# Decoding the weights in place, scaling the first output weights once, and pooling q and k of eight pairs on TensorE

## The chip, the core and the metric

The kernel runs on one core of a Trainium2 chip. The metric is the device time of one execution in microseconds (us), the median of the runs. Engines are named as the profile names them: PE is TensorE (PEld its weight loads), DVE VectorE, ACT ScalarE, POOL GpSimd, and SP the engine that issues the DMAs (SPq its queue). TensorE's clock has two levels, 1.2 and 2.4 GHz; the profile gives the granted clock as a share of the higher one.

## What is computed

Three steps follow one another: an attention over 4 batches of 8 heads, whose output becomes 2304 tokens of 512 numbers, and two MLPs (called moe) of 512 to 2048 to 512.

```python
def _attn_ref(q, k, v):                       # (4, 8, 576, 64)
    ...
    q_d = q.reshape(B, H, Sd, factor, D).mean(axis=3)      # factor 4, Sd 144
    k_d = k.reshape(B, H, Sd, factor, D).mean(axis=3)
    v_d = v.reshape(B, H, Sd, factor, D).mean(axis=3)
    out_d = sm_attn(q_d, k_d, v_d)            # softmax(q k^T / 8) v
    out_up = np.repeat(out_d, factor, axis=2)
    mask = np.abs(pos[:, None] - pos[None, :]) < factor
    scores = np.where(mask, scale * np.matmul(q, k.transpose(0, 1, 3, 2)), -1000000000.0)
    ...                                       # softmax over the masked scores
    return (out_up + np.matmul(attn, v)).astype(np.float32)

def _moe_ref(x, w_in, w_out):
    h = x @ w_in
    g = np.maximum(h, 0.0) + np.log1p(np.exp(-np.abs(h)))
    return (g @ w_out).astype(np.float32)

def _moe2_ref(x, w_in, w_out):
    h = x @ w_in
    g = h * np.cos(h)
    return (g @ w_out).astype(np.float32)
```

## The kernel before

**Attention.** The heads are taken two at a time: 16 pairs (b, c), b the batch and c a pair of heads. `pair` (L525) writes one pair as a chain of named operations. qk, vd and vw are its loads (L528, L531, L533). sum1 and sum2 pool q and k by fours on DVE, into `qt` and then `qd`; sum3 and sum4 pool v, in place in `vd` and then into `vs`. A are the masked local scores on PE, A2 to A6 their softmax on DVE and ACT (`nm`, `sm`, `rs`). B are the scores of the pooled heads (three fp32 matmuls, L630), B1 to B4 their softmax, with B1a a scaling of the maximum `nd`. C and D are transposes on PE into PSUM, copied to `aT` and `aTd`; E are the products with v; up and E1 add the two outputs into `xt`, the tokens of the next step.

**MLPs.** Every fp32 operand is split into a high and a low f16 half after a scaling by powers of two, and each product is three f16 matmuls (high by high, high by low, low by high). L1 is x by w_in of the first MLP (L897, weights `w1i`), L2 its g by w_out (L989, `w1o`), L3 and L4 the same of the second (L897 with `w2i`, L1031 with `w2o`). Tokens go in five tiles, four of 512 and one of 256, and each tile through 16 units f of 128 hidden channels; a unit is 12 L1 or L3 matmuls, a chain of activations on ACT and DVE (`ta`, `tb`, `td`, `g`), and 12 L2 or L4 matmuls that add into two PSUM banks. L2 and L4 of a unit follow `LAG` = 4 units later (8 for the last tile).

**Weights.** They come as float64 bit patterns, in eight blocks b of 1024 columns for each of the four matrices. `Weight.decode` takes a block: a load into one of two staging buffers `stg` (L440, 1 MB), rebase on ACT (L453), join1 and join2 on DVE (L339 and L461) into one of three buffers `x`, and bound on ACT (L467), which gives each row's maximum in `bd`. join2 is the last reader of `stg`, bound writes a throw-away copy into the place of the high halves. `Weight.scale` spreads `bd` over all partitions (a matmul with an identity on PE, L378, and a reduction on DVE, L385) and finds the power of two by a few small steps on DVE; `Weight.split` writes the high half (L354 on ACT or L356 on DVE) and the low half (L350 on DVE). W1I and both matrices of the second MLP are scaled block by block. W1O is scaled in four groups of two blocks; so the first tile of L2 is accumulated in four parts, which `y_out` adds up on DVE (L1011).

**Scale of a tile.** Before a tile enters L1 or L3, its largest value is spread in the same way (`tile_scale`, `am`), and the four pieces of `xt` are split (`split_x`). In the second MLP `y_in(t)` does this at the start of tile t, and before tile 4 `drain(0)` empties the list of waiting L4 units.

**Order.** A planner (`Plan.due`, `Plan.order`) gives every operation a due time, going back from the end along the dependencies, and then lists the operations of each engine by due time and modelled cost; each engine executes its list in that order. While PE is idle in the plan, `filler` (L1195) puts zero matmuls there. Buffers in rings are given out in that order too, so a load waits on SP until its buffer is free.

Of the kernel before, what the change touches and what calls it, by code (L numbers as in the profile page):

```python
# [44 lines left out]
NQK, NVD, NVW, NSM, NXB, NST, NGS = 3, 2, 3, 3, 3, 2, 8  # L45
# [10 lines left out]
W2STEP = 1  # L56
# [27 lines left out]
class Plan:  # L84
# [36 lines left out]
    def due(self):  # L121
        nxt = 0.0
        for op in reversed(self.ops):
            e, cost = min(op.cost.items(), key=lambda x: x[1])
            end = min([s.due - LAT[e] for s in op.succ], default=0.0)
            if "pe" in op.cost:
                end = min(end, nxt)
                nxt = end - cost
            op.due = end - cost
# [26 lines left out]
    def order(self):  # L156
# [12 lines left out]
        def cool(cost, weight):  # L169

            if now < 0.6 or now > WARM:
                return False
            a0 = now + cost - WIN
            busy[:] = [b for b in busy if b[1] > now - WIN]
            return cost * weight + sum(max(0.0, b - max(a, a0)) * w for a, b, w in busy) < THR
# [91 lines left out]

def dma(kb):
    return {"sp": kb / 353.0}


def build(tc, qk, vw, vd, mask, w1i, w1o, w2i, w2o, out):
# [3 lines left out]
    with ExitStack() as ctx:  # L276
# [12 lines left out]
        def carr(name, n=1):  # L289
            return const.tile([128, n], F32, name=name)  # L290
# [6 lines left out]
        vmx = const.tile([128, NC_], F32, name="vmx")  # L297
# [17 lines left out]
        XB, STG = ring(dp, "x", NXB, [128, 2, 512]), ring(dp, "stg", NST, [128, 2, 512], I64)  # L315
# [52 lines left out]
        def allmax(am, n, red, reads, writes, name):  # L368
# [20 lines left out]
            P.add(pe(0.3 * n), spread, reads, [h], [h], name + " spread")  # L389
# [24 lines left out]
        class Weight:  # L414
            def __init__(self, name, dram):
                self.name, self.dram = name, dram
                self.w = [None] * NF
                self.bd, self.s = carr(f"bd_{name}", NB), carr(f"s_{name}", NF)

            def place(self, pool_):  # L420
                self.t = pool_.tile([128, NF, 2, 512], F16, name=f"{self.name}_t")

            def hi(self, f, a, n):
                return self.t[:, f, 0, a : a + n]

            def lo(self, f, a, n):
                return self.t[:, f, 1, a : a + n]
# [7 lines left out]
            def decode(self, b, after=()):  # L435

                raw, x = STG_.new(), XB_.new()
# [9 lines left out]
                def rebase():  # L447
# [6 lines left out]
                        out=x.t, in_=half(F32, 1), func=AF.Prelu, scale=float(2.0**-112), alpha=-float(2.0**32)  # L454
                    )

                def join1():
                    ts(bits(x.t), bits(x.t), 3, ALU.logical_shift_left)

                def join2():  # L460
                    nc.vector.scalar_tensor_tensor(  # L461
                        out=bits(x.t), in0=half(I32, 0), scalar=29, in1=bits(x.t),
# [9 lines left out]
                P.add(act(1024), rebase, [raw], [x], [x], nm + " rebase")  # L472
# [3 lines left out]
                return x  # L476
# [15 lines left out]
            def split(self, b, x):  # L492
                w, s = lambda: self.t[:, 2 * b : 2 * b + 2], self.s[:, 2 * b : 2 * b + 1]
                k = ("s", self.name, b)
# [5 lines left out]
                P.add(  # L500
                    dve(1024, False, 1), lambda: less("dve", w()[:, :, 1, :], x.t, s, w()[:, :, 0, :]),
                    [x, k], self.keys(b), name=nm + " low",
# [5 lines left out]
        STG_, XB_ = STG, XB  # L508
# [752 lines left out]
```

## Time and profile before

| what | before |
|---|---|
| median of 3 runs | 947.76 us (947.12 to 948.87) |
| the profiled execution | 947.95 us, span 946.2 us |
| granted clock of PE, mean | 0.986 |
| busy PE, DVE, ACT | 899.2, 690.4, 470.0 us |
| first L2 matmul, first L3 matmul | 173.70, 541.99 us |
| zero matmuls | 205, 53.07 us |

The span is the time from the first to the last instruction of the profiled execution. In the tables of windows a row is one stretch of it, with the busy time of each engine and the number of its instructions in brackets. Timelines list instructions, or runs of equal ones, with their start and length; in square brackets stand the idle time of the engine ahead of them and what ended it. A name with an arrow reads output<-inputs. Matmuls of fp32 leave two records each.

### The profile page before, as it was taken

How to read it: one execution, taken by the hardware profiler on the slowest of the kernel's cores; microseconds unless marked ns; L12 is line 12 of the kernel's file. 1: busy time of each engine (PE TensorE's matmuls, PEld its weight loads, DVE VectorE, ACT ScalarE, POOL GpSimd, SP SyncE). 2: the span in 40 equal slices, each digit the busy share in tenths (PEclk: the TensorE clock that was granted, in tenths of full speed). 3: DMA queues.
4: the chain of work that ended last, by engine and by line, in shares of the span. 5: the costliest groups of instructions: out<-in, count | busy, mean ns of one | idle time of the engine just before them, and what ended most of it. 6: DMA issues, size and time to landing. Idle time of an engine off the chain costs nothing.

```text
span 946.2 us, 14558 instructions
## 1 busy us (share of the span) xinstructions
PE 899.2 (95%) x5809; PEld 469.7 (50%) x5809; DVE 690.4 (73%) x1474; ACT 470.0 (50%) x823; POOL 1.6 (0%) x11
## 2 busy tenths in 40 slices
PE   7899887799999999999999999999999999999797
PEld 4555443345555554444446864444444444444364
DVE  7999999976668776999964566567557656755465
ACT  3464696525445467879866632234224323422243
POOL 0000000000000000000000000000000000000000
PEclk9999998899999999999999999999999999999899
DMA  9557332400122003442200000010001000100100
GB/s 312 164 168 243 119 128 89 171 26 27 31 64 104 1 1 118 152 175 89 90 1 1 1 2 0 1 42 4 1 1 45 1 1 1 45 1 1 44 1 23
DMA packets 13363, 58.89 MB, mean 62 GB/s; under 512 B 1520, under 2 KB 1648, under 8 KB 9200
## 3 DMA queue, kind: packets, MB, share of 16 engines
q1 hardware_dynamic: 13296, 57.97, 17.7%
q8 instruction: 45, 0.74, 0.3%
q14 instruction: 22, 0.18, 0.1%
HBM read 53.25 MB, written 4.72 MB: 61 GB/s over the span
## 4 chain that ended last, share of the span: by engine, by line
PE 74%; DVE 16%; ACT 6%; DMA 2%; issue 1%; SPq 0%; ACTq 0%; DVEq 0%
PE h L897 34%; PE any L1031 19%; PE any L989 17%; DVE td L350 1%; DVE x L461 1%; PE any L724 1%; DVE sm L342 1%; DVE w1i_t L350 1%; DMA vd<-vd 1%; ACT ta L905 1%; DVE xt L350 1%; DMA qk<-qk 1%; DVE rs L602 1%; PE any L675 1%; DVE g L342 1%
## 5 line engine op out<-in xcount | busy, mean ns | idle before, releaser
L897 PE MATMUL h<-xt,w2i_t 128*128 128x512 f16 (+1 forms) x960 | 201.5, 362 | 9.5 <-DVE xt L866 5.3
L897 PE MATMUL h<-xt,w1i_t 128*128 128x512 f16 (+1 forms) x960 | 199.4, 360 | 9.3 <-DVE red L385 6.6
L1031 PE MATMUL any<-w2o_t,g 128*128 128x512 f16 x864 | 197.1, 379 | 0.3 <-DVE g L362 0.3
L989 PE MATMUL any<-g,w1o_t 128*128 128x512 f16 (+1 forms) x864 | 179.5, 357 | 2.3 <-ACT ed L646 1.4
L897 PEld LDWEIGHTS <-w2i_t 128*128 128x128 f16 x960 | 95.3, 99 | 105.7 <-issue 11.5
L897 PEld LDWEIGHTS <-w1i_t 128*128 128x128 f16 x960 | 93.8, 98 | 102.6 <-issue 14.2
L989 PEld LDWEIGHTS <-w1o_t 128*128 128x128 f16 x960 | 93.7, 98 | 89.1 <-issue 4.8
L930 ACT ACTIVATE ta<-h,quarter,i 128x512 f32<-128x512 f32 (+1 forms) x80 | 58.8, 735 | 155.2 <-PE h L897 155.2
L1031 PEld LDWEIGHTS <-g 128*128 128x128 f16 x864 | 84.5, 98 | 100.6 <-DVE g L362 0.8
L342 DVE TENSOR_TENSOR g<-td,g 128x512 f16<-128x512 f32 (+1 forms) x152 | 96.3, 634 | 8.0 <-ACT g L360 1.3
L905 ACT ACTIVATE ta<-h,i 128x512 f32<-128x512 f32 (+1 forms) x80 | 51.4, 642 | 80.7 <-PE h L897 67.4
L935 DVE TENSOR_SCALAR tb<-ta 128x512 f32<-128x512 f32 (+1 forms) x80 | 32.0, 400 | 77.6 <-ACT ta L930 77.1
L945 DVE SCALAR_TENSOR_TENSOR td<-h,r,tc 128x512 f32<-128x512 f32 (+1 forms) x80 | 55.8, 697 | 42.9 <-ACT tc L941 41.2
L941 ACT ACTIVATE tc<-ta 128x512 f32<-128x512 f32 (+1 forms) x80 | 46.9, 586 | 74.5 <-DVE ta L342 74.5
L350 DVE SCALAR_TENSOR_TENSOR td<-ta,sg,tb 128x512 f32<-128x512 f32 (+1 forms) x64 | 43.7, 682 | 48.4 <-ACT ta L917 48.0
L917 ACT ACTIVATE ta<-ta,one 128x512 f32<-128x512 f32 (+1 forms) x80 | 54.2, 680 | 2.0
L362 DVE CAST g<-td 128x512 f16<-128x512 f32 (+1 forms) x124 | 49.4, 398 | 8.0 <-PE any L989 0.8
L342 DVE TENSOR_TENSOR ta<-ta,tb 128x512 f32<-128x512 f32 (+1 forms) x80 | 51.0, 638 | 2.4
L909 ACT ACTIVATE tb<-h,r 128x512 f32<-128x512 f32 (+1 forms) x80 | 51.1, 639 | 0.0
L913 ACT ACTIVATE ta<-ta 128x512 f32<-128x512 f32 (+1 forms) x80 | 46.9, 588 | 0.0
L453 ACT ACTIVATE x<-stg 128x1024 f32<-128x1024 f32 x32 | 36.8, 1149 | 14.1 <-DVE w2i_t L350 3.8
L1195 PE MATMUL h<-zero 128*128 128x512 f16 x133 | 34.4, 393 | 5.3 <-POOL zero L1186 2.4
(147 smaller groups left out, 848.8 us busy)
## 6 DMA issues: line engine op xcount, KB each, us to landing
qk<-qk SPq DMA_DIRECT2D x16, 589.0 KB, 6.6
stg<-w1i SPq DMA_DIRECT2D x8, 1024.0 KB, 7.0
stg<-w1o SPq DMA_DIRECT2D x8, 1024.0 KB, 6.4
stg<-w2i SPq DMA_DIRECT2D x8, 1024.0 KB, 4.8
stg<-w2o SPq DMA_DIRECT2D x8, 1024.0 KB, 4.8
vw<-vw SPq DMA_DIRECT2D x16, 320.0 KB, 4.3
vd<-vd SPq DMA_DIRECT2D x16, 288.0 KB
out<-osb SPq DMA_DIRECT2D x18, 256.0 KB, 2.1
```

Source lines behind the costliest of these rows:

```text
L342: eng[e].tensor_tensor(out=out, in0=in0, in1=in1, op=op)
L350: nc.vector.scalar_tensor_tensor(out=out, in0=raw, scalar=s, in1=other, op0=ALU.mult, op1=op)
L362: nc.vector.tensor_copy(out, in_)
L897: nc.tensor.matmul(h.t[:, 0:n], l, r, start=(i == 0), stop=(i == 11))
L905: act(n, 1, True), lambda: nc.scalar.activation(out=a(), in_=h.t[:, 0:n], func=AF.Abs, scale=col(o.i1, f)),
L909: act(n, 1, True), lambda: nc.scalar.activation(out=b(), in_=h.t[:, 0:n], func=AF.Relu, scale=col(o.r1, f)),
L913: act(n), lambda: nc.scalar.activation(out=a(), in_=a(), func=AF.Exp, scale=-1.0),
L917: act(n, 1), lambda: nc.scalar.activation(out=a(), in_=a(), func=AF.Ln, bias=one),
L930: act(n, 2, True), lambda: nc.scalar.activation(out=a(), in_=h.t[:, 0:n], func=AF.Identity, scale=col(o.i2, f), bias=quarter), [h, *sc], [ ...
L945: dve(n, False, 1), lambda: nc.vector.scalar_tensor_tensor(out=td.t[:, 0:n], in0=h.t[:, 0:n], scalar=col(o.r1, f), in1=r(), op0=ALU.mult, ...
L989: nc.tensor.matmul(a.t[:, i, 0:n], l, r, start=(first and j == 0), stop=(last and j == 2))
L1031: nc.tensor.matmul(a.t[:, i], l, r, start=(f == 0 and j == 0), stop=(f == NF - 1 and j == 2))
```

## The change

Weights are decoded in place. The f32 values of block b lie over the place of the low halves of block b and of the high halves of block b+1, in a tile that is one unit longer; the ring `x` is gone. bound's throw-away copy goes into the staging buffer, which is so given back after bound. The high of block b waits for the low of block b-1. W1I is scaled in two groups of four blocks. All eight blocks of W1O are decoded first and scaled once (`first_scale`), and the first tile of L2 is accumulated in one go. The second MLP's matrices are scaled in groups of two.

For batches 0 and 1 (eight pairs) q and k are pooled by PE: `sums`, eight fp32 matmuls with the identity for each pair, accumulated in PSUM, and `place`, three copies on ACT, the last with B1a's scale. The other pairs' B1a goes to ACT. Copies of the pairs of batches 0 and 1, the highs of W1I and W1O and of some x go to ACT always. The operands of the spreads become bf16.

In the second MLP the scale of tile t+1 is asked for at unit 8 of tile t, and before tile 4 four units stay in the list. The planner's due times take each engine's capacity into account, its costs are changed, and the zero matmuls come out as 82 instead of 205.

```diff
-W2STEP = 1
+W2STEP = 2
+W2G = 2
+QKP, VP = (0, 1), ()
+YIN = 8
+DR4 = 4
+A_W, A_C, A_X, A_G = True, True, True, False
+OUT0 = 10
+IN0 = ((0, 4), (4, 4))
...
-        ident_s = const.tile([128, 128], F32, name="ident_s")
+        ident_s = const.tile([128, 128], BF16, name="ident_s")
...
-                self.t = pool_.tile([128, NF, 2, 512], F16, name=f"{self.name}_t")
+                self.t = pool_.tile([128, 1024 * (NF + 1)], F16, name=f"{self.name}_t")
...
+            def floats(self, b):
+                return self.t[:, 2048 * b + 1024 : 2048 * b + 3072].bitcast(F32).rearrange("p (m e) -> p m e", m=2)
...
-                raw, x = STG_.new(), XB_.new()
+                raw, x = STG_.new(), ("float", self.name, b)
...
                 def bound():
-                    nc.scalar.activation(
-                        out=self.t[:, 2 * b : 2 * b + 2, 0, :].bitcast(BF16), in_=x.t, func=AF.Abs,
-                        accum_out=self.bd[:, b : b + 1],
-                    )
+                    out = raw.t.rearrange("p m e -> p (m e)")[:, 0:256].bitcast(BF16)
+                    with nc.allow_low_precision(reason="a bound, for the choice of a scale"):
+                        nc.scalar.activation(
+                            out=out.rearrange("p (m e) -> p m e", m=2), in_=self.floats(b), func=AF.Abs,
+                            accum_out=self.bd[:, b : b + 1],
+                        )
...
-                P.add(act(1024, 1), bound, [x], [("bd", self.name, b), *self.keys(b)], name=nm + " bound")
+                P.add(act(1024, 1), bound, [x], [("bd", self.name, b), raw], name=nm + " bound")
...
+                over = [("float", self.name, b - 1)] if b else []
                 P.add(
-                    {**act(1024, 1), **dve(1024, True, 1)}, lambda e: scaled(e, w()[:, :, 0, :], x.t, s),
-                    [x, k], self.keys(b), name=nm + " high",
+                    either(act(1024, 1), dve(1024, True, 1), self.first and A_W), lambda e: scaled(e, self.his(b), self.floats(b), s),
+                    [x, k], self.keys(b) + over, name=nm + " high",
                 )
...
+                def sums():
+                    x = tk.t[:, :, 3 : 3 + S].rearrange("p a (i r) -> p a i r", r=4)
+                    for a in range(2):
+                        for r in range(4):
+                            nc.tensor.matmul(
+                                hst()[:, SD * a : SD * a + SD], ident, x[:, a, :, r], start=(r == 0), stop=(r == 3)
+                            )
+
+                def place():
+                    for j in range(2):
+                        h = slice(64 * j, 64 * j + 64)
+                        copy("act", qd.t[h, SD * j : SD * j + SD], hst()[h, 0:SD])
+                    nc.scalar.activation(
+                        out=qd.t[:, 2 * SD : 3 * SD], in_=hst()[:, SD : 2 * SD], func=AF.Copy, scale=float(2.0**-7)
+                    )
...
-        def grp_out(g):
-            xs = [W1O.decode(2 * g), W1O.decode(2 * g + 1)]
+        def grp_out():
+            for b in range(NB):
+                W1O.decode(b)
+            W1O.scale(0, 4)
+            first = [("sc0", b) for b in range(NB)]
             W1O.scale(
-                2 * g, 2, group_scale(g), [("sc0", 2 * g), ("sc0", 2 * g + 1)],
-                [("sc0g", g)] + [("s", "w1o", 2 * g), ("s", "w1o", 2 * g + 1)],
+                4, 4, first_scale(), first + [("s", "w1o", b) for b in range(4)],
+                [("sc", 0)] + [("s", "w1o", b) for b in range(NB)],
             )
-            for i in range(2):
-                W1O.split(2 * g + i, xs[i])
+            for b in range(NB):
+                W1O.split(b)
...
         for i, (k, t, f) in enumerate(seq2):
-            if f == 0:
-                if t == 4:
-                    drain(0)
+            if i == 0:
                 y_in(t)
+            if f == YIN and t < 4:
+                y_in(t + 1)
+            if t == 4 and f == 0:
+                drain(DR4)
```

At three places of DVE's list the order stands as follows. The first is the start of the program. Before, with the sums of q and k (`qt`, `qd`) of the first pairs:

```order
L342 TENSOR_TENSOR qt_119<-qk_111 128x288 x2
L342 TENSOR_TENSOR qd_120<-qt_119 64x144 x2
L342 TENSOR_TENSOR qd_120<-qt_119 128x144
L342 TENSOR_TENSOR vd_114<-vd_114 72x4x128
L560 TENSOR_REDUCE vmx<-vw_116 128x1
L342 TENSOR_TENSOR vs_122<-vd_114 72x256
L593 TENSOR_REDUCE nm_220<-any_87 128x10
L342 TENSOR_TENSOR qt_119<-qk_112 128x288 x2
```

The same place on DVE after:

```order
L383 TENSOR_TENSOR vd_111<-vd_111 72x4x128
L383 TENSOR_TENSOR vs_119<-vd_111 72x256
L648 TENSOR_REDUCE vmx<-vw_113 128x1
L679 TENSOR_REDUCE nm_219<-any_87 128x10
L383 TENSOR_TENSOR vd_112<-vd_112 72x4x128
L383 TENSOR_TENSOR sm_122<-any_87,nm_219 128x640
L722 TENSOR_REDUCE nd_227<-h_91 96x3
```

The sums of q and k are gone from DVE, and its first operation is now the sum of v.

The second place is the scaling of W1O ahead of the first low half that L2 needs. Before, on DVE, for the first group of two blocks (`gs`, `kg`, `ikg` are the steps of that group, `x` the decoded blocks):

```order
L810 TENSOR_TENSOR gs<-lc_159,s_w1o 128x4
L350 SCALAR_TENSOR_TENSOR td_96<-ta_93,lc_159,tb_95 128x512
L811 TENSOR_REDUCE kg<-gs 128x1
L350 SCALAR_TENSOR_TENSOR xt_83<-xt_83,sx_179,xs_97 128x512
L339 TENSOR_SCALAR ikg<-kg 128x1
L342 TENSOR_TENSOR xt_84<-td_96,xt_84 128x512
L339 TENSOR_SCALAR s_w1o<-lc_159,kg 128x4
L866 COPY xt_83<-xs_97 128x512
L356 TENSOR_SCALAR w1o_t<-x_106,s_w1o 128x2x512
L356 TENSOR_SCALAR xs_97<-xt_83,sx_179 128x512
L350 SCALAR_TENSOR_TENSOR w1o_t<-x_106,s_w1o,w1o_t 128x2x512
```

The same place on DVE after, for all eight blocks:

```order
L896 TENSOR_TENSOR gs<-lc_160,s_w1o 128x16
L391 SCALAR_TENSOR_TENSOR td_96<-ta_93,lc_160,tb_95 128x512
L897 TENSOR_REDUCE k_166<-gs 128x1
L403 CAST xt_85<-td_96 128x512
L380 TENSOR_SCALAR ik_167<-k_166 128x1
L383 TENSOR_TENSOR xt_85<-td_96,xt_85 128x512
L380 TENSOR_SCALAR s_w1o<-lc_160,k_166 128x16
L391 SCALAR_TENSOR_TENSOR td_96<-ta_92,lc_160,tb_94 128x512
L694 RECIPROCAL rs_223<-rs_223 128x10
L740 TENSOR_SCALAR sd_231<-sd_231 96x3
L403 CAST xt_86<-td_96 128x512
L383 TENSOR_TENSOR sm_124<-sm_124,rs_223 128x640
```

The steps are over 16 columns instead of 4, the high half is no longer on DVE, and the first low half (L391 with w1o_t) comes right behind the last row.

The third place is the scale of tile 4 in the second MLP (`sx_215` before, `sx_216` after). Before, on DVE, it stands behind the last outputs of tile 3 (`osb`):

```order
L362 CAST g_105<-td_96 128x512
L342 TENSOR_TENSOR g_105<-td_96,g_105 128x512
L356 TENSOR_SCALAR osb_4391<-any_89,ik_202 128x512
L356 TENSOR_SCALAR osb_4393<-any_88,ik_202 128x512
L385 TENSOR_REDUCE red<-h_91 128x1
L339 TENSOR_SCALAR sx_215<-red 128x1
L339 TENSOR_SCALAR sx_215<-sx_215 128x1
L339 TENSOR_SCALAR c_4_211<-sx_215 128x1
```

After, on DVE:

```order
L1021 TENSOR_SCALAR tb_95<-ta_93 128x512
L383 TENSOR_TENSOR ta_93<-ta_93,tb_95 128x512
L1031 SCALAR_TENSOR_TENSOR td_96<-h_91,r_3_198,tc_4404 128x512
L426 TENSOR_REDUCE red<-h_90 128x1
L380 TENSOR_SCALAR sx_216<-red 128x1
L380 TENSOR_SCALAR sx_216<-sx_216 128x1
L383 TENSOR_TENSOR g_105<-td_96,g_105 128x512
L380 TENSOR_SCALAR c_4_212<-sx_216 128x1
```

It moved between two units of tile 3, ahead of that tile's last outputs.

## Rows read from the trace of the kernel before

**Rows 1.** Windows by stage: us, length, busy PE, PEld, DVE, ACT, POOL, PEclk, DMA, GB/s.

```profile
0.00:167.20 167.20, 143.33 (x1496) 82.74 (x1496) 157.70 (x376) 101.88 (x201) 1.64 (x11) 0.98 0.52 173
167.20:173.70 6.50, 0.79 (x2) 0.53 (x3) 6.50 (x14) 4.49 (x11) 0.00 (x0) 0.68 0.37 115
173.70:542.00 368.30, 365.28 (x2384) 196.04 (x2384) 280.76 (x596) 232.10 (x408) 0.00 (x0) 1.00 0.19 66
542.00:887.90 345.90, 343.17 (x1641) 160.65 (x1639) 210.75 (x393) 111.38 (x160) 0.00 (x0) 1.00 0.03 10
887.90:904.40 16.50, 9.75 (x46) 5.92 (x45) 9.72 (x36) 4.96 (x10) 0.00 (x0) 0.69 0.17 64
904.40:946.20 41.80, 36.93 (x247) 23.78 (x245) 24.96 (x64) 15.17 (x34) 0.00 (x0) 0.98 0.04 14
```

**Rows 2.** Windows, the zero matmuls (L1195) alone: length, busy PE, PEld, PEclk.

```profile
0.00:173.70 173.70, 51.44 (x199) 18.55 (x199) 0.97 0.51 171
```

**Rows 3.** PE's timeline at the first L2: start, us, engine, line, [idle before <-releaser].

```profile
171.49 0.79 PE L378 MATMUL h<-ident_s,bd_w1o 128*128 128x128 f32 x2 [5.61 <-ACT w1o_t L467]
173.70 7.48 PE L989 MATMUL any<-g,w1o_t 128*128 128x512 f16 x28 [1.42 <-ACT ed L646]
```

**Rows 4.** PE's timeline in the second MLP, at starts of tiles.

```profile
641.83 5.34 PE L897 MATMUL h<-xt,w2i_t 128*128 128x512 f16 x24 [0.92 <-DVE td L945]
...
891.53 0.49 PE L897 MATMUL h<-xt,w2i_t 128*128 128x256 f16 x3 [3.25 <-DVE xt L866]
...
900.29 2.72 PE L897 MATMUL h<-xt,w2i_t 128*128 128x256 f16 x12 [1.48 <-DVE td L945]
```

**Rows 5.** DVE's timeline, in three short stretches of the opening.

```profile
4.63 0.83 DVE L342 TENSOR_TENSOR qt<-qk 128x288 f32<-128x288 f32 x2 [3.73 <-DMA qk<-qk]
...
29.77 1.21 DVE L461 SCALAR_TENSOR_TENSOR x<-stg,x 128x1024 int32<-128x1024 int32 x1
30.90 0.81 DVE L342 TENSOR_TENSOR sm<-any,nm 128x640 f32<-128x640 f32 x1
...
59.39 0.16 DVE L652 TENSOR_SCALAR sd<-sd 96x3 f32<-96x3 f32 x1
...
59.67 1.19 DVE L461 SCALAR_TENSOR_TENSOR x<-stg,x 128x1024 int32<-128x1024 int32 x1
```

**Rows 6.** DVE's groups from 0 to 167.2: xcount | busy us, mean ns.

```profile
L461 DVE SCALAR_TENSOR_TENSOR x<-stg,x 128x1024 int32<-128x1024 int32 x11 | 13.3, 1211 | 0.0
...
L342 DVE TENSOR_TENSOR qt<-qk 128x288 f32<-128x288 f32 x20 | 8.2, 451 | 3.9 <-DMA qk<-qk 3.9
L342 DVE TENSOR_TENSOR sm<-any,nm 128x640 f32<-128x640 f32 x10 | 8.1, 810 | 0.0
...
L339 DVE TENSOR_SCALAR x<-x 128x1024 int32<-128x1024 int32 x11 | 7.5, 685 | 0.0
...
L342 DVE TENSOR_TENSOR qd<-qt 64x144 f32<-64x144 f32 x20 | 5.9, 297 | 0.1
...
L362 DVE COPY aTd<-any 72x576 f32<-72x576 f32 x5 | 3.7, 747 | 0.3 <-PE any L692 0.3
```

**Rows 7.** Page, landing of W1O's loads, and ACT's bound from 0 to 167.2.

```profile
stg<-w1o SPq DMA_DIRECT2D x8, 1024.0 KB, 6.4
...
L467 ACT ACTIVATE w1i_t<-x 128x1024 bf16<-128x1024 f32 x8 | 8.5, 1059 | 7.7 <-DVE x L461 7.7
```

**Rows 8.** PE's timeline, pooled scores B, then the transposes C.

```profile
72.53 0.90 PE L630 MATMUL any<-qd 128*96 128x144 f32 x6
73.26 0.71 PE L675 MATMUL any<-ident,sm 128*128 128x128 f32 x5
```

**Rows 9.** Windows, the spreads (L378) alone: length, busy PE, PEld, PEclk.

```profile
173.70:946.20 772.50, 10.69 (x56) 9.84 (x56) 0.99 0.11 38
```

**Rows 10.** Windows of PE alone: length, busy PE, PEclk, DMA, GB/s.

```profile
144.00:148.00 4.00, 0.00 (x0) 0.70 0.48 135
148.00:152.00 4.00, 3.67 (x9) 0.50 0.93 389
```

More of the change, by code (lines that the diff above doesn't have):

```diff
@@ L121, in due @@
     def due(self):
[L122 to L129, printed above, removed]
+        pre = {op: [] for op in self.ops}
+        for op in self.ops:
+            for x in op.succ:
+                pre[x].append(op)
+        left = {op: len(op.succ) for op in self.ops}
+        end = {op: 0.0 for op in self.ops}
+        free = dict.fromkeys(("pe", "dve", "act", "pool", "sp"), 0.0)
+        pes = [op for op in self.ops if "pe" in op.cost]
+        ready = [op for op in self.ops if not left[op] and "pe" not in op.cost]
+        n = len(self.ops)
+        while n:
+            best = None
+            cand = list(ready)
+            if pes and not left[pes[-1]]:
+                cand.append(pes[-1])
+            for op in cand:
+                for e in op.cost:
+                    x = (min(free[e], end[op]) if e in CAP else end[op], op.n)
+                    if best is None or x > best[0]:
+                        best = (x, op, e)
+            (x, _), op, e = best
+            if op is (pes[-1] if pes else None):
+                pes.pop()
+            else:
+                ready.remove(op)
+            op.due = x - op.cost[e]
+            if e in CAP:
+                free[e] = op.due
+            n -= 1
+            for q in pre[op]:
+                end[q] = min(end[q], op.due - LAT[min(q.cost, key=lambda z: q.cost[z])])
+                left[q] -= 1
+                if not left[q] and "pe" not in q.cost:
+                    ready.append(q)
         first = {}
@@ L172, in cool @@
                 return False
+            cost = min(cost, 2.4)
             a0 = now + cost - WIN
@@ L507, in build @@
         W1O.place(wp)
-        STG_, XB_ = STG, XB
+        STG_ = STG
+        raw0 = [dp.tile([128, 512], F32, name=f"raw{c}") for c in range(NC_)]
         att_ops = []
@@ L641, in B1a @@
             def B1a():
-                nc.vector.tensor_scalar_mul(nd.t[0:RB, 0:3], nd.t[0:RB, 0:3], float(2.0**-7))
+                nc.scalar.activation(
+                    out=nd.t[0:RB, 0:3], in_=nd.t[0:RB, 0:3], func=AF.Copy, scale=float(2.0**-7)
+                )
             def B2():
@@ L712, in Em @@
                     for k in range(2):
[L713 to L716 removed]
+                        vp = [tv.t[:, 2 * j + k, r, :] for r in range(4)] if b in VP else [vs.t[:, 2 * j + k, :]]
+                        for i, v in enumerate(vp):
+                            nc.tensor.matmul(
+                                po.t[64 * j : 64 * j + 64, 1, u0 : u0 + SD], v, aTd.t[:, k, SD * j : SD * j + SD],
+                                start=(k == i == 0), stop=(k == 1 and i == len(vp) - 1),
+                            )
                 for n in range(2 * NG):
@@ L1087, in build @@
         for f in range(NF):
-            if f % 2 == 0:
-                grp_in(f // 2)
+            if f // 2 in dict(IN0) and f % 2 == 0:
+                grp_in(f // 2, dict(IN0)[f // 2])
+            if f == OUT0:
+                grp_out()
             unit_in(1, 0, f)
             step()
-        for g in range(4):
-            grp_out(g)
         for f in range(NF):
@@ L1111, in place2 @@
             dp2 = ex.enter_context(tc.tile_pool(name="dp2", bufs=1))
-            for s, n, shape, dt in ((STG2, NST2, [128, 2, 512], I64), (XB2, NXB2, [128, 2, 512], F32)):
-                s.tiles += [dp2.tile(shape, dt, name=f"{s.name}{i}") for i in range(n)]
+            STG2.tiles += [dp2.tile([128, 2, 512], I64, name=f"stg2{i}") for i in range(NST2)]
         def place3():
@@ L1152, in second @@
                 P.add({"sp": 0.01}, place2, [], ["place2"], [], "place2", after=done)
-                STG_, XB_ = STG2, XB2
+                STG_ = STG2
             for _ in range(min(n, len(todo))):
                 W, b = todo.pop(0)
-                x = W.decode(b, after=[P.wrote["place2"]])
-                W.scale(b, 1)
-                W.split(b, x)
+                W.decode(b, after=[P.wrote["place2"]])
+                if b % W2G == W2G - 1:
+                    W.scale(b - W2G + 1, W2G)
+                    for a in range(b - W2G + 1, b + 1):
+                        W.split(a)
         for i, (k, t, f) in enumerate(seq):
```

181 lines of the change are left out of this document (94 added, 87 removed).

## The prediction

> **What bounds the kernel now.** I read the windows by stage first [rows 1]. Their columns are the length of the stretch, then the busy time of PE, PEld, DVE, ACT and POOL, the granted clock, the DMA share and GB/s. From 173.7 us on TensorE works nearly without a gap: 365.28 of 368.30 us, then 343.17 of 345.90. Those two stages get shorter only by less TensorE work. The gain must come from three other places.
>
> The first is the opening, up to the first matmul with W1O at 173.7. There DVE is busy 157.70 of 167.20 us, while PE's 143.33 hold 199 zero matmuls up to L2's start [rows 2], 51.44 us of recorded time, that no result needs. DVE bounds this stretch. What comes last is in PE's timeline [rows 3]: the spread of the next W1O group's maxima stands in PE's queue ahead of the first L2 matmul, PE waits 5.61 us there for the bound of that group on ACT, and L2 begins at 173.70. The second place is the stretch from 887.9 to 904.4, where tile 4's scale is found: 16.50 us with 9.75 of PE busy at a granted clock of 0.69 [rows 1]. The third is a 0.92 us wait at the start of a tile in the second MoE [rows 4], of which there are three.
>
> **Part 1, the opening on DVE.** Neighbouring DVE records overlap: an operation of 1.21 us is followed after 1.13, and three small ones, the first recorded at 0.16, take 0.28 in all [rows 5]. So I price an operation at its mean less 0.07, a small one at 0.09. Up to the end of the first W1O low DVE does about 156.5 us of work before (157.70, less the second low). By the changed order, up to the same operation:
> - pooled sums: 16 fewer of 0.38 and 27 fewer of 0.27 (two thirds of them 64 rows high) [rows 6]: -13.3
> - scale steps of W1I for two groups instead of eight: 42 small operations fewer at 0.09, larger reductions +0.3: -3.5
> - copies and highs forced to ACT: 20 operations, the dearest aTd at 0.68, 0.48 on average: -9.7
> - work no longer ahead of this point: one pair's attention (9 operations, up to the 0.74 of sm), 8 operations of units in L1 and 6 of the splits of x, 0.51 on average: -11.7
> - all eight W1O blocks are now decoded before it, 16 joins of each kind instead of 11: 5 x (1.14 + 0.61) [rows 6]: +8.7
>
> Sum -29.5, so 127 us. DVE loses some time at the start: its first operation, which waited 3.73 us for q and k until 4.63 [rows 5], is gone, and the first that remains needs vd, which came a little later; together with the wait for the first scores I take 6.3. DVE alone would end at 133.
>
> **Part 1, the staging chain.** In-place decoding puts a new wait on SP: a staging buffer is given back after ACT's bound, no longer after join2. Queued behind that load on SP are the next pairs' q, k and v. One turn of one of the two buffers is 6.4 (landing of W1O), twice 1.06 for ACT's passes [rows 7], 0.61 and 1.14 for the joins: 10.3 us. The time queued behind other work on SP, DVE and ACT comes on top; I take 12.5. In the changed order 57.9 us of DVE work end with the sixth join2, at 64.2 with the start; the sixteenth is five turns later, at 126.7. DVE's own work would bring it at 121.5, so the chain is late by some 5 us. Behind it stand the last spread, the steps and 11.8 us of DVE work up to the first low: L2 begins at about 140, between 134 (DVE alone with its last hand-over) and 152 (turns of 15). The 5.61 us wait goes, since no W1O spread stands between. I take 140, near DVE's bound, because that is what the rows price. Gain **33.7**.
>
> ACT gets five rebases and bounds, the places, copies and highs: some 15 us more than the 101.88 of the first window [rows 1], below DVE's 127. It is free in time only on average: its queue is in order, and a bound behind a copy that waits for PE delays a load.
>
> **Part 1, PE.** The 64 added matmuls are fp32, 144 columns. Three of that size (two records each) took 0.73 us, from 72.53 to the next record at 73.26 [rows 8], so 0.245 each: +15.7, hidden, because fillers shrink from 199 to 77 in the changed order: 102 us of work and 16.6 of fillers are 119, below 140. Bounds: 0.06 if a column passed at the f16 rate (24 L3 matmuls of 512 columns take 5.2 us [rows 4], so 0.216 each), which changes nothing, and 0.49 at twice the row. Here the moving operand is read with a step of four fp32, which no row of PE shows; the nearest strided row is DVE's own sum1 on the same tile, pairs out of every four, 288 elements in 0.45 [rows 6], at no more per element than the 640 of sm in 0.81. I take 0.245 and keep 0.49 as a rival. The Trainium skill, "SBUF — State Buffer", Door 1 (DMA port swizzle), speaks against the change: it says SBUF has 16-byte cachelines, that full bandwidth needs at least two hits in a line, and that an access that crosses to a new line pays a penalty. A step of 16 bytes has one hit in each line; sum1's pairs have two, so its row does not contradict the page. With no penalty the sum stands; with one of the size of rival A the end is at about 903.
>
> **Part 2, PE's work behind 173.7.** The 28 spread matmuls there (two records each) are recorded at 10.69 us in fp32 [rows 9], some 9.2 without the overlap of records. 25 remain, in bf16; at a quarter of the 0.216 of 512 columns they take 1.5, so -7.7 (bounds -10.7 and 0). One pair's attention more lies behind L2's start: +2.9. Together **-4.8**. The other matmuls are the same in number and shape, so the small losses between them stay.
>
> **Part 3, the second MoE.** The scale of tile t+1 is now found in the middle of tile t, and tile 4 no longer drains the queue first. The 16.50 us hold 36 L3 matmuls of 0.11, six L4 of 0.22 and two spreads, 5.5 us at full clock: **-11.0**. There PE waited 3.25 us for a split of x, 1.48 for the activation at its end [rows 4], and shorter ones between, and worked at a granted clock of 0.69 [rows 1]. The three waits of 0.9 go: **-2.7**. Next late is nothing: four L4 units remain in the queue as cover. What stands behind the last matmul (scaling and storing) stays.
>
> **Sum.** 946.2 - 33.7 - 4.8 - 11.0 - 2.7 = 894.0 of span. The profiled execution took 947.95 for a span of 946.2, so 1.75 lies around it: 895.7 against its own time, and 0.2 less against the median of 947.76: **895.5**.
>
> **Rivals.**
> (A) *The strided sums cost twice the row.* PE's work in the opening is 134 with fillers, and PE and DVE wait for each other: L2 at about 148, end 903.5. For: no row shows this access. Against: sum1's row.
> (B) *The staging chain takes the gain.* Turns of 14 to 16 us, with longer landings and SP's queue standing behind ACT: the sixteenth join2 at 134 to 144, L2 at 147 to 157, end 902.5 to 912, middle 907. For: the new wait on an in-order queue. Against: only 5 turns hang on it.
> (C) *The end part does not do what it says*, tile 4 still waits because DVE reaches the scale late: 11.0 stay, 906.5. Against: the changed order has the reduction between two units of tile 3.
> (D) *Slower: the clock.* From 144 to 148 PE did nothing and the granted clock was 0.70; from 148 to 152 it worked at 0.50, the 1.2 GHz level [rows 10]. 122 fillers go. If PE's 102 us of work ran at 0.50 throughout, with 33 us of waits, the opening would take 237 and the end be at 992. It decides above an L2 start of 192, that is with over 57 of the 102 us at the low level. Against: the opening's clock was 0.98 [rows 1], real matmuls now stand where fillers stood, and DVE's 140 hides the first 40 us of it.
>
> **How the numbers follow.** Forecast 64%, own range 886 to 902 (L2 between 134 and 147, spreads at 0 to -10.7). A 13%, B 13%, C 4%, D 3%, and 3% for under 886, where the chain costs nothing and DVE is better filled at the start. The range 884 to 914 takes in A, B, C and the unknown costs and leaves out some 9%, D and the ends. A measurement here can tell about 0.2% from no change; only D, or several mishaps at once, comes near that: faster 0.96, same 0.01, slower 0.03.
>
> **What would show it.** First L2 matmul near 140, with DVE busy over 90% ahead of it and no wait for a spread before it; the pooled sums at 2 us per pair on PE (4 would be A); loads of W1O under 13 us apart for one buffer (B if over 14); granted clock of the opening above 0.9 (D if near 0.6); no gap above 1 us at tile 4's start, and 754 us from the first L2 matmul to the end instead of 772.5. A first L2 after 155 makes the forecast wrong.

## The result and the profile after

The changed kernel takes 907.17 us (906.71 to 909.23), against 947.81 for the kernel before (now the median of four runs): a ratio of 0.9575, 95% interval 0.9557 to 0.9592. The profiled execution took 906.71 us for a span of 904.9.

The page's busy times, and the windows by stage (columns as in [rows 1]; the first cut is the first L2 matmul, which stood at 173.70 before [rows 3]):

```profile
PE 890.0 (98%) x5772; PEld 474.8 (52%) x5772; DVE 646.9 (71%) x1311; ACT 486.3 (54%) x878; POOL 1.6 (0%) x11
```

```profile
0.00:154.20 154.20, 144.56 (x1434) 94.30 (x1435) 129.31 (x253) 116.75 (x244) 1.64 (x11) 0.97 0.61 206
154.20:532.00 377.80, 377.07 (x2536) 204.27 (x2535) 279.86 (x573) 244.41 (x440) 0.00 (x0) 1.00 0.17 59
532.00:860.00 328.00, 328.00 (x1555) 151.76 (x1553) 213.98 (x426) 110.99 (x167) 0.00 (x0) 1.00 0.03 10
860.00:904.90 44.90, 40.38 (x253) 24.45 (x251) 23.73 (x62) 14.14 (x29) 0.00 (x0) 1.00 0.09 36
```

The opening is 19.5 us shorter (173.70 to 154.22), what stands behind it 21.8 (772.5 to 750.7). From 154.2 on PE has hardly a gap, and the stretch of 16.50 us at tile 4's start [rows 1] is gone. In the opening the bound has changed: DVE is busy 129.31 of 154.20 us where it was 157.70 of 167.20 [rows 1], and PE 144.56, though the zero matmuls fell from 199 [rows 2] to 77 (21.38 us recorded). The reason is in PE's timeline. These are the pooling matmuls of the second and fifth pair, two records to a matmul, and the first L2 matmuls:

```profile
11.09 4.26 PE L627 MATMUL h<-qk,ident 128*128 128x144 f32 x16
...
45.47 4.30 PE L627 MATMUL any<-qk,ident 128*128 128x144 f32 x16
...
154.22 1.46 PE L1074 MATMUL any<-g,w1o_t 128*128 128x512 f16 x6
```

Eight matmuls take 4.1 us up to the start of the next record (4.3 by their own), 0.52 each, where those of the pooled scores with as many columns take 0.245 [rows 8]. All 64 together, from the windows of that line, and what ACT waited for in the opening (us in all, times, longest):

```profile
0.00:154.20 154.20, 34.57 (x128) 26.23 (x128) 0.97 0.61 206
```

```profile
ACT qd L401 <- PE h L627: 10.5, 4, 6.7
ACT qd L401 <- PE any L627: 7.6, 3, 3.6
```

ACT stands 18 us in its queue ahead of `place` until the sums are done. What is behind it there, among it rebase and bound of the weights, waits along. Of the first 77 us of the chain of waits the pooling matmuls alone hold 38% (22.2 and 16.1 on the two kinds of banks); before, loads and many kinds of DVE operations shared that stretch, the largest with 11%.

### The profile page after: what moved, and what is told of

It is laid out like the page before. It is cut to its first block, busy times and chain, and to the rows that moved or that the text cites. A ratio compares the mean times of both kernels' runs of the same rounds, so it can differ in the third digit from the quotient of the medians.

```text
span 904.9 us, 14336 instructions
## 1 busy us (share of the span) xinstructions
PE 890.0 (98%) x5772; PEld 474.8 (52%) x5772; DVE 646.9 (71%) x1311; ACT 486.3 (54%) x878; POOL 1.6 (0%) x11
## 4 chain that ended last, share of the span: by engine, by line
PE 88%; DVE 5%; ACT 4%; DMA 2%; issue 1%
PE h L983 37%; PE any L1109 21%; PE any L1074 19%; PE any L815 2%; PE h L627 2%; PE any L627 2%; PE h L1285 1%; DVE w1o_t L391 1%; PE any L804 1%; DMA stg<-w1i 1%; PE any L662 1%; DVE td L391 1%; PE any L764 1%; PE any L716 1%; PE any L781 1%; ACT stg L524 1%
## 5 line engine op out<-in xcount | busy, mean ns | idle before, releaser
L983 PE MATMUL h<-xt,w2i_t 128*128 128x512 f16 (+1 forms) x960 | 199.0, 358 | 0.0
L391 DVE SCALAR_TENSOR_TENSOR td<-ta,sg,tb 128x512 f32<-128x512 f32 (+1 forms) x64 | 43.6, 682 | 52.1 <-ACT ta L1003 51.3
L391 DVE SCALAR_TENSOR_TENSOR xt<-xt,sx,xs 128x512 f16<-128x512 f32 (+1 forms) x36 | 24.8, 688 | 3.7 <-ACT xs L395 3.5
L395 ACT ACTIVATE xs<-xt,sx 128x512 f16<-128x512 f32 (+1 forms) x27 | 18.4, 680 | 14.6 <-DVE xt L952 12.5
```

The lines of the kernel that those rows point to most:

```text
L391: nc.vector.scalar_tensor_tensor(out=out, in0=raw, scalar=s, in1=other, op0=ALU.mult, op1=op)
L983: nc.tensor.matmul(h.t[:, 0:n], l, r, start=(i == 0), stop=(i == 11))
```

## The experiments

Theory S says that the step of four fp32 doubles the price of the pooling matmuls, so that PE and, through it, ACT set the opening. Rival B says that the longer hold of the staging buffers does. All times below are medians, and "L2 at" is the first L2 matmul of the profiled execution. How far that point moves by itself is shown by two sets of runs with the same lists, row for row: 154.22 in the first, 157.61 in the other (fourth experiment). The run with the end part undone has the same lists up to 539 us, and L2 at 157.21.

**Neighbouring columns in the pooling matmuls.**

```diff
-        hst()[:, SD * a : SD * a + SD], ident, x[:, a, :, r], start=(r == 0), stop=(r == 3)
+        hst()[:, SD * a : SD * a + SD], ident, tk.t[:, a, 3 + SD * r : 3 + SD * r + SD], start=(r == 0), stop=(r == 3)
```

> The changed kernel with one edit: the moving operand of the 64 pooling matmuls is 144 neighbouring columns instead of every fourth one (it sums other elements of q and k, so the pooled scores are not the reference's). Number, size and order of the instructions stay. Theory S, the step of 16 bytes doubles these matmuls and PE was thereby late for the first L2 matmul: a pair's eight take 2.0 to 2.2 us instead of 4.1, the first L2 matmul moves from 154.2 to 140 to 146, the time from 907 to 893 to 899. Rival B, the chain of staging buffers sets the first L2 matmul: the eight get as cheap, but L2 begins at 151 to 154 and the time stays above 903. Rival P, the price is that of fp32 with accumulation in PSUM and has nothing to do with the step: still 4.1 us a pair and 907.

Measured: 900.43 us (898.99 to 902.7), ratio 0.9488 [0.9464, 0.9511] where the changed kernel has 0.9575: 6.7 us less, with the same instructions in the same order. PE's timeline, the second pair and L2, the window up to L2, and ACT's wait for the sums there:

```profile
10.86 2.13 PE L627 MATMUL h<-qk,ident 128*128 128x144 f32 x16
...
148.59 1.46 PE L1074 MATMUL any<-g,w1o_t 128*128 128x512 f16 x6
```

```profile
0.00:148.59 148.59, 127.81 (x1435) 83.52 (x1436) 128.85 (x253) 116.58 (x244) 1.64 (x11) 0.99 0.64 214
```

```profile
ACT qd L401 <- PE h L627: 6.5, 1, 6.5
```

The price halves (2.1 to 2.2 us for seven of the pairs, 3.97 for the first), PE is busy 16.8 us less and ACT waits 6.5 us for the sums instead of 18; rival P falls. L2 comes 5.6 us earlier, which is a third of what PE saved and 2.6 us short of S's range. So the step costs what S says, but something else stands close behind PE.

**The price of the step by itself.**

```diff
+                    step = {(0, 0): 1, (0, 1): 2, (0, 2): 3, (0, 3): 4, (1, 0): 2, (1, 1): 3, (1, 2): 1, (1, 3): 4}[b, c]
...
+                            o = 3 + (SD if step == 1 else 1) * r
...
-                                ident, x[:, a, :, r], ...
+                                ident, tk.t[:, a, o : o + step * (SD - 1) + 1 : step], ...
```

> The changed kernel with other steps in the moving operand of the pooling matmuls, one for each of the eight pairs in the order of the program: for batch 0 steps of 1, 2, 3 and 4 fp32, for batch 1 of 2, 3, 1 and 4 (it sums other elements, so the pooled scores are not the reference's). It measures the price of the step by itself. Theory S as the Trainium skill's line of 16 bytes with two hits would have it: 2.1 us for the eight matmuls at steps 1 and 2, 4.1 at 3 and 4. Rival: the price grows with each byte of step, so that 2 lies near 2.8 and 3 near 3.4.

PE's timeline, four of the eight pairs, with steps of 2, 3, 1 and 4:

```profile
44.23 2.28 PE L628 MATMUL any<-qk,ident 128*128 128x144 f32 x16
48.81 3.29 PE L628 MATMUL any<-qk,ident 128*128 128x144 f32 x16
61.66 2.13 PE L628 MATMUL any<-qk,ident 128*128 128x144 f32 x16
96.31 4.27 PE L628 MATMUL any<-qk,ident 128*128 128x144 f32 x16
```

The other batch has 2.22 at a step of 2, 3.34 at 3 and 4.36 at 4 (its first pair, step 1, 2.60). A step of two fp32 costs next to nothing, three half as much again, four twice. Neither side had all of it: S had 4.1 at a step of 3, the rival 2.8 at a step of 2. The trace agrees with the Trainium skill ("SBUF — State Buffer", Door 1), which says that SBUF has 16-byte lines and that full bandwidth needs two hits in a line; it gives no size of the penalty. Four elements at a step of 2 touch two lines, at 3 three and at 4 four, and the measured prices stand as 2 to 3 to 4. The same place of the Trainium skill gives four fp32 as how far one can stride for free; read as a step, that is not so here: the measurement says two. The time was 904.22 (one run), between the two neighbours.

**The staging buffers' hold.** Two runs, since the first changed more than it meant to. Both let bound write into a tile of its own; in the first the planner knew it.

```diff
-                    out = raw.t.rearrange("p m e -> p (m e)")[:, 0:256].bitcast(BF16)
+                    out = junk
...
-                P.add(act(1024, 1), bound, [x], [("bd", self.name, b), raw], name=nm + " bound")
+                P.add(act(1024, 1), bound, [x], [("bd", self.name, b)], name=nm + " bound")
```

> The changed kernel, but bound writes its throw-away copy into a tile of its own, so that a staging buffer is given back after join2 as in the kernel before. Rival B, the longer hold of the staging buffers delays the last W1O block: L2 begins 4 to 8 us earlier and the time is 899 to 903. Theory S, PE with the dear pooling is what comes last: within 2 us of 907.

Measured 918.59 us (ratio 0.9671), slower by 11. L2 is at 154.99, but 24 L1 matmuls more stand behind it: the planner had made other lists, and PE is busy 755.2 us behind L2 instead of 745.4. It says nothing on the hold. The second leaves the planner's line as it is, and only the store changes:

> The run with bound's own store again, but with the planner's lists left as they are in the changed kernel (in the earlier run the planner had rewritten them, and 24 L1 matmuls more stood behind the first L2). The only difference on the chip is that a staging buffer is free after join2 instead of after bound. Rival B, the longer hold delays the opening: each turn of a buffer 1.5 to 4 us shorter, L2 begins 3 to 8 us before 154.2, time 899 to 904. Theory S, PE's dear pooling and the ACT operations behind it come last: L2 within 2 us of 154.2, time 905 to 909.

Measured 906.56 us, ratio 0.9551 [0.953, 0.9572], L2 at 154.11. The loads do go out earlier (the first of W1O at 87.44 us instead of 90.28), and yet L2 stays. DVE's timeline of this run has the sixth and the sixteenth join2:

```profile
76.82 1.19 DVE L516 SCALAR_TENSOR_TENSOR w1i_t<-stg,w1i_t 128x1024 int32<-128x1024 int32 x1
...
139.92 1.22 DVE L516 SCALAR_TENSOR_TENSOR w1o_t<-stg,w1o_t 128x1024 int32<-128x1024 int32 x1
```

That is (141.14 - 78.01) / 5 = 12.6 us for a turn of one buffer, and the changed kernel has 12.8. The hold is not what the opening waits for. To see whether it is what stands behind PE, the same with neighbouring columns:

> Neighbouring columns in the pooling matmuls (as in the first run, other elements are summed) and bound's own store with unchanged lists (as in the fifth) together. Each alone moved L2's start to 148.6 and to 154.1, from 154.2. Theory: with PE out of the way the longer hold of the staging buffers is what is left of the delay, L2 at 141 to 145, 893 to 897. Rival: the rest is not the hold but what the lists and the landings make DVE and ACT wait for at the start and between W1I's blocks, L2 at 147 to 149, 899 to 902.

Measured 899.72 us (897.05 to 902.52) and L2 at 148.82, against 900.43 and 148.59 without it; a turn takes 12.1 us, against 12.2. PE works here at a granted clock of 0.50 to 0.66 from 120 to 132 us, where the other run has 1.00, so a small gain could be hidden; the several microseconds that rival B stands for are in neither place.

**More zero matmuls.**

```diff
-            cost = min(cost, 2.4)
```

> The changed kernel with the planner's rule for zero matmuls as it was before (the cap of 2.4 us on a matmul group's weight taken out): 137 zero matmuls ahead of the first L2 instead of 77, everything else in its lists as close as the planner leaves it. In the changed kernel PE idles at 122 to 125 us and works at a granted clock of 0.50 from 126 to 137. Theory C, that dip costs about 4 us of the 14 by which L2 is late: granted clock above 0.9 there, L2 2 to 5 us earlier, 902 to 905. Rival: more zero matmuls take PE's time in an opening that PE bounds, 908 to 912.

The edit left every list as it was, with 77 zero matmuls and not 137. So this is the changed kernel once more: 909.01 us (907.18 to 912.98), L2 at 157.61. It tells nothing on the clock, but how far apart two sets of runs of one kernel lie here: about 2 us, with L2 3.4 us apart.

**One part undone: all pooling on DVE.**

```diff
-QKP, VP = (0, 1), ()
+QKP, VP = (), ()
```

> One part undone: q and k of all pairs are pooled on DVE as before (QKP empty), everything else of the change stays. Theory S: PE loses 34 us of pooling in the opening and is no longer late, DVE gets 13 us back and bounds with the staging chain: L2 begins at 148 to 154, the time is 901 to 907, so that the pooling on PE bought next to nothing at its real price. Rival: pooling on PE pays even at 4.1 us a pair, L2 begins after 160 without it and the time is above 912.

Measured 906.05 us (905.42 to 908.65), ratio 0.955 [0.9527, 0.9572], L2 at 155.92: the time is in S's range, L2 is 1.9 us behind it. The pooling on PE, as written, buys nothing: the changed kernel has 907.17. The lists are other ones here, with 144 zero matmuls ahead of L2 instead of 77, so two whole kernels are compared. Why DVE can have it back shows in the first windows. All pooling on DVE:

```profile
0.00:12.00 12.00, 8.61 (x110) 4.57 (x110) 6.63 (x17) 3.81 (x11) 1.64 (x11) 1.00 0.84 257
12.00:28.00 16.00, 12.18 (x151) 8.05 (x151) 13.48 (x34) 7.57 (x18) 0.00 (x0) 1.00 0.95 325
28.00:48.00 20.00, 18.92 (x254) 12.35 (x253) 19.91 (x49) 9.89 (x28) 0.00 (x0) 0.91 0.58 185
```

The changed kernel, with one window more:

```profile
0.00:12.00 12.00, 9.49 (x73) 6.70 (x74) 3.57 (x8) 2.65 (x6) 1.64 (x11) 1.00 0.85 275
12.00:28.00 16.00, 16.00 (x195) 12.07 (x194) 13.02 (x28) 9.23 (x26) 0.00 (x0) 1.00 0.84 289
28.00:48.00 20.00, 19.97 (x227) 15.20 (x226) 16.17 (x32) 11.69 (x28) 0.00 (x0) 1.00 0.84 274
48.00:77.00 29.00, 28.57 (x261) 19.64 (x261) 25.34 (x55) 21.88 (x54) 0.00 (x0) 1.00 0.37 119
```

Up to 48 us DVE does 40.0 us of work with the pooling and 32.8 without, 7.3 less in the same time: it waits there for loads, for PE and for ACT. PE meanwhile is busy 35.97 of the 36 us from 12 to 48.

**The pooling in smaller portions.** Four pairs on PE (`QKP = (0,)`); the eight with the first addition left on DVE, so that PE reads in steps of two; and the planner told the real price.

> Only the four pairs of batch 0 are pooled on PE, those of batch 1 on DVE as before. PE has 17 us less in the opening, DVE some 6.7 more, ACT 3.5 less. Theory S with a second bound close behind (the run with neighbouring columns gained 6 us of PE's 17): 901 to 905, better than eight pairs on PE (907) and none (906). Rival: DVE is as late as PE and nothing is gained, 906 to 909.

Measured 910.68 us, ratio 0.96 [0.9573, 0.9626], L2 at 152.88 with one pair's transposes more ahead of it.

```diff
-                        for r in range(4):
+                        for r in range(2):
...
+                aop({"dve": 0.74}, sum1, [tk], [qt], [qt], nm + "sum1")
-                aop(pe(2.3), sums, [tk, "ident"], [hs], [hs], "sums " + nm)
+                aop(pe(1.1), sums, [qt, "ident"], [hs], [hs], "sums " + nm)
```

> The eight pairs' pooling shared: DVE adds the pairs as before (sum1, 0.75 us a pair more on DVE), PE adds the two halves with the identity, four matmuls a pair with a step of two fp32 instead of eight with a step of four. By the price of the step that the run with other steps showed, a pair takes 1.1 us on PE instead of 4.1, 25 us less in the opening. If PE's dear pooling and ACT's waiting for it were most of what was late: 899 to 904. Rival: DVE's 6 us more and the staging loads eat it, 905 to 910.

Measured 912.29 us, ratio 0.9635 [0.9599, 0.967], L2 at 157.56, although most pairs now take on PE what was expected, the second one for instance:

```profile
10.01 1.18 PE L627 MATMUL h<-qt,ident 128*128 128x144 f32 x8
```

DVE is busy 143.9 us ahead of L2 then, where the changed kernel has 129.3, and PE 130.4; one more pair's transposes stand ahead of L2 here too.

```diff
-                aop(pe(2.3), sums, [tk, "ident"], [hs], [hs], "sums " + nm)
+                aop(pe(4.2), sums, [tk, "ident"], [hs], [hs], "sums " + nm)
```

> The changed kernel with the planner told that a pair's pooling takes 4.2 us on PE instead of 2.3, so that it orders around the real price. Theory S: part of what the dear matmuls cost was waiting of ACT for them (18 us in the opening) because the lists assumed half the price; L2 begins 2 to 6 us earlier, 901 to 905. Rival: PE's work is what it is, the order can't hide it, within 2 us of 907.

Measured 912.42 us, ratio 0.9617 [0.9591, 0.9642]. L2 is 2.8 us earlier, but 24 L1 matmuls moved behind it, and later PE waits twice for 1.7 us. All three of these expectations failed. The three have other lists than the changed kernel all through, and I can't separate the edit from the lists in them; what they show is that none of these ways beats it.

**The end part undone.**

```diff
+            if f == 0:
+                if t == 4:
+                    drain(0)
+                y_in(t)
-            if i == 0:
-                y_in(t)
-            if f == YIN and t < 4:
-                y_in(t + 1)
-            if t == 4 and f == 0:
-                drain(DR4)
```

> The end part undone: in the second MLP the scale of a tile is found at its start again, and before tile 4 the list of L4 units is emptied; the rest of the change stays. My sum put this part at 13.7 us: 918 to 922, with a stretch of some 16 us at tile 4's start and three waits of 0.9. Rival: other parts of the change (the order) had filled these waits already, 908 to 914.

Measured 920.62 us, ratio 0.9703 [0.9678, 0.9728]. Behind L2 (157.21) it takes 763.9 us to the end of its span of 921.1, the changed kernel 750.7: the part is worth 13.2 us. PE's timeline has the waits of [rows 4] back, one of the three at a tile's start and the first at tile 4:

```profile
618.97 5.35 PE L983 MATMUL h<-xt,w2i_t 128*128 128x512 f16 x24 [0.92 <-DVE td L1031]
...
868.33 0.80 PE L983 MATMUL h<-xt,w2i_t 128*128 128x256 f16 x3 [3.41 <-DVE xt L952]
```

**The spreads in fp32 again.**

```diff
-        ident_s = const.tile([128, 128], BF16, name="ident_s")
+        ident_s = const.tile([128, 128], F32, name="ident_s")
...
-                self.bd, self.s = carr(f"bd_{name}", NB, BF16), carr(f"s_{name}", NF)
+                self.bd, self.s = carr(f"bd_{name}", NB), carr(f"s_{name}", NF)
...
```

> The changed kernel with the spreads' operands in fp32 as before (identity, bounds and maxima), order as in the changed kernel. It measures part 2 of the prediction: 25 spreads behind the first L2 matmul cost PE 7 us more there (4.0 us recorded in bf16, some 10 in fp32), the opening is not longer: 912 to 916. Rival: the spreads lie in PE's queue where it has slack, under 2 us, 905 to 909.

Measured 913.19 us, ratio 0.9626 [0.9607, 0.9644], 6.0 more than the changed kernel. Windows of the spreads alone behind L2, in the changed kernel, then with fp32:

```profile
154.20:904.90 750.70, 4.01 (x25) 2.41 (x25) 1.00 0.10 36
```

```profile
156.20:911.20 755.00, 8.16 (x50) 7.87 (x50) 1.00 0.11 36
```

Behind L2 the difference is 4.3 us (755.0 to 750.7), as the records have it (8.16 less 4.01); the rest is in an L2 at 156.23, within what that point moves by itself. What one spread costs shows where the next matmul starts, in the changed kernel, then with fp32:

```profile
155.51 0.22 PE L419 MATMUL h<-ident_s,am 128*128 128x128 bf16 x1
155.57 4.48 PE L1074 MATMUL any<-g,w1o_t 128*128 128x512 f16 x20
```

```profile
157.52 0.38 PE L419 MATMUL h<-ident_s,am 128*128 128x128 f32 x2
157.75 0.59 PE L1074 MATMUL any<-g,w1o_t 128*128 128x512 f16 x2
```

It takes PE 0.06 us in bf16 and 0.23 in fp32; the rest of the records runs beside the next matmul.

## Why the prediction was right, and where it was off

The time lies in the range and the sign was right, but 907.2 is not the 895.5 of the likeliest case and lies outside the forecast's own range of 886 to 902; the stated range held because it was drawn to take in rivals A and B. It is rival A's price that came, the sums at twice the row, 4 us a pair. L2 is at 154, where A had about 148 and B 147 to 157: the time and L2 alone would fit B as well, and only the runs on the step and on the hold tell them apart.

Of the signs that the prediction named, the opening's clock (0.97), the missing gap at tile 4 and the 750.7 us behind L2 (754 foretold) came. DVE is busy 84% of the time ahead of L2 and not over 90, the loads of W1O into one buffer stand 10.4 to 14.4 us apart, on both sides of the 13, and L2 missed 140. A first L2 after 155 was to make the forecast wrong: 154.22 is short of that by 0.8 us, and in the second set of runs of the same lists it is 157.61. That the time stayed within 12 us of the forecast is in part luck, since the stretch behind L2 gave 3.3 us more than foretold. By the steps of the prediction:

- *DVE's work in the opening.* Predicted 127 us up to the first low. Measured 129.31 to 154.2, which holds the low and a little more. Right.
- *PE's sums.* Taken at 0.245 each, measured 0.52. This is the term that was mis-sized: 34 us of recorded PE time instead of 15.7. sum1's row [rows 6] was no neighbour of this access: it reads two neighbours out of every four and the pooling matmuls one, and one out of every two costs next to nothing on PE either (2.2 us).
- *The start.* 6.3 us were taken for what DVE waits at the start, and the sixth join2 to end at 64.2. It ended at 77.33, with DVE busy 58.10 of the first 77 us, so the 57.9 us of work were right and the waiting was 19. Neighbouring columns bring that end to 73.3. This is DVE's timeline of the changed kernel at the sixth and the sixteenth join2, then that with neighbouring columns:

```profile
76.14 1.19 DVE L516 SCALAR_TENSOR_TENSOR w1i_t<-stg,w1i_t 128x1024 int32<-128x1024 int32 x1
...
140.03 1.22 DVE L516 SCALAR_TENSOR_TENSOR w1o_t<-stg,w1o_t 128x1024 int32<-128x1024 int32 x1
```

```profile
72.04 1.28 DVE L516 SCALAR_TENSOR_TENSOR w1i_t<-stg,w1i_t 128x1024 int32<-128x1024 int32 x1
...
133.06 1.22 DVE L516 SCALAR_TENSOR_TENSOR w1o_t<-stg,w1o_t 128x1024 int32<-128x1024 int32 x1
```

- *The staging chain.* Five turns of 12.5 us were predicted from there; measured (141.25 - 77.33) / 5 = 12.8, with neighbouring columns (134.28 - 73.32) / 5 = 12.2. From the last join2 to L2 13.3 were predicted and 13.0 measured (14.3 with neighbouring columns). So 13.1 of the 14.2 us by which L2 is late were lost before the sixth join2, 4.0 of them by the step; between it and the sixteenth the step costs 3 us more. The sixth join2 moves by itself too (79.92 in the second set of runs of the same lists), so these shares are those of one pair of executions. The turns came out as priced, but the hold until bound, which the prediction made part of them, changes nothing when it is taken away (12.6 and 12.1 us).
- *What is left.* With cheap sums L2 is still 8.6 us later than 140. In the chain of waits of that run loads hold 31 of the first 50 us, most of the rest are ACT passes behind them (start, us, what):

```profile
2.96 8.06 DMA vd<-vd
...
14.10 11.35 DMA stg<-w1i
...
28.53 5.57 DMA stg<-w1i
...
39.68 6.17 DMA stg<-w1i
```

  The second staging block, asked for right behind the first, takes 11.35 us to land where 6.4 [rows 7] was priced for each. The windows of that run have the 16 DMA engines busy 0.85 to 0.98 of the time, and PE, with the cheap sums, 15.33 of the 20 us from 28 on:

```profile
0.00:12.00 12.00, 9.23 (x79) 7.09 (x80) 3.71 (x8) 2.65 (x6) 1.64 (x11) 1.00 0.85 262
12.00:28.00 16.00, 15.64 (x215) 11.57 (x213) 13.99 (x29) 10.08 (x28) 0.00 (x0) 1.00 0.98 318
28.00:48.00 20.00, 15.33 (x252) 12.23 (x251) 16.27 (x33) 11.69 (x28) 0.00 (x0) 1.00 0.85 274
```

  The prediction allowed DVE 6.3 us of waiting at the start. It idles 8.3 us up to 12 us here and 5.7 more up to 48, since with the pooling gone it has too little else to do while the first loads come. That the loads are the cause of the whole 8.6 us is argued from the chain; no run made them faster.
- *The clock.* PE idles for 2.30 us ahead of 124.96 and then works at the 1.2 GHz level for some 10 us, from 126 on (windows of PE alone as in [rows 10], then two runs of its timeline):

```profile
124.00:128.00 4.00, 3.04 (x29) 0.79 0.45 147
128.00:132.00 4.00, 4.00 (x42) 0.50 0.83 307
132.00:136.00 4.00, 3.22 (x9) 0.50 0.70 231
```

```profile
124.96 1.24 PE L1285 MATMUL any<-zero 128*128 128x512 f16 x5 [2.30 <-ACT aT L401]
...
132.78 4.60 PE L983 MATMUL h<-xt,w1i_t 128*128 128x512 f16 x12 [0.78 <-DVE red L426]
```

  Twelve L1 matmuls take 4.60 us there against 2.76 at full clock. This is rival D in small. What this stretch costs at L2 stays open, since the run meant for it changed nothing. In other runs such a stretch stands right ahead of L2, where its price can be read from the 36 L1 matmuls there: first in the changed kernel, at a granted clock of 1.00, then with neighbouring columns, then in the second set of runs of the same lists, each of these two with the window that has the lower clock:

```profile
146.45 7.93 PE L983 MATMUL h<-xt,w1i_t 128*128 128x512 f16 x36
```

```profile
139.85 8.89 PE L983 MATMUL h<-xt,w1i_t 128*128 128x512 f16 x36
```

```profile
140.00:144.00 4.00, 4.00 (x16) 0.78 0.22 88
```

```profile
148.49 9.28 PE L983 MATMUL h<-xt,w1i_t 128*128 128x512 f16 x36
```

```profile
148.00:152.00 4.00, 4.00 (x13) 0.60 0.34 133
```

  So the clock takes 1.0 us of L2's start with neighbouring columns and 1.4 of the 3.4 us by which two sets of runs of one kernel differ. D at large did not come: the opening's granted clock is 0.97 with 77 zero matmuls.
- *Behind L2.* Predicted -18.5, measured -21.8. The end part was put at 13.7 and is worth 13.2. The spreads were put at -7.7, from 9.2 in fp32 to 1.5 in bf16. The 0.06 us for one in bf16 was right, the fp32 side was mis-sized: its records [rows 9] run beside the next matmuls, and the 25 spreads are worth 4.3 us by the run that undid them. Another 2.3 lie in gaps that had been taken as staying: 3.0 us of idle PE from L2 to the second MLP [rows 1] became 0.7. With the 2.9 of one more pair, as priced, some 5 us of the 21.8 are left that no run assigns; three spreads fewer are among them.

In sum: 895.5, plus 14.2 for L2, less 3.3 behind it, is 906.4; the remaining 0.8 is that the median lies 2.3 above the span here and 1.5 in the sum.

Of the 40.6 us gained, 13.2 are thus the end part, some 4 the bf16 spreads, and 17.8 of the 19.5 us in the opening come without the pooling on PE too, since the kernel without it is as fast (L2 at 155.92). How those divide among the single scaling of W1O, the decoding in place, the operations forced to ACT and the planner's new due times is not shown: no run undid one of them.

## What to carry to other kernels

Before moving a sum to TensorE, look at the step of its moving operand: here, with fp32, two elements apart cost next to nothing and four apart doubled the matmul, and a row of another engine on the same tile did not tell it. Price a small matmul by when the next one starts, since its record runs on beside that one. Work taken from an engine in a stretch in which it will wait for loads anyway buys little; price the waiting anew once the work is gone, from the loads. Where a planner writes the order, an edit and the lists it leads to have to be kept apart: hold the lists still when a cause is to be tested (a truer cost made this kernel 5 us slower by other lists).

## What was new of the hardware

The fp32 matmul's price by the step of its moving operand, eight of 144 columns: 2.13 us at 1, 2.2 to 2.3 at 2, 3.3 at 3, 4.3 at 4. Between two sets of runs of the same lists the opening differed by 3.4 us and the median by 1.8.
